# Attention and maxout on one core: first banks, weight differences and row sums put in another order

## The chip, the cores and the metric

The kernel runs on one core of one Trainium2 chip. The core has a matrix engine (TensorE, PE in the profile; its weight loads are shown apart as PEld), VectorE (DVE), ScalarE (ACT), GpSimd (POOL) and SyncE (SP). The engines run side by side, each through its own list of instructions in a fixed order, and wait for each other by semaphores. Transfers run on 16 DMA engines and are issued here by POOL and SP. TensorE writes its products to PSUM, which has eight banks of 128 partitions by 512 fp32 numbers; another engine must read a bank out before TensorE may fill it again. SBUF is the on-chip memory from which all engines read.

The metric is the device time of one execution in microseconds (us).

## The reference

The input is q, k, v of 8 batches, 8 heads, 1024 positions and 64 channels, two projections E and F of 64 x 1024, and three weights. Linformer attention is followed by a two-way maxout layer, all in fp32:

```python
k_proj = einsum('ks,bhsd->bhkd', E, k)      # 1024 positions -> 64
v_proj = einsum('ks,bhsd->bhkd', F, v)
scores = (q @ k_proj^T) / 8                 # 1024 x 64 for each head
attn   = exp(scores - max) ; attn /= sum(attn) + 1e-9
x      = (attn @ v_proj), heads side by side  # 8192 tokens x 512
out    = maximum(x @ w1, x @ w2) @ w_out      # 512 -> 1024 -> 512
```

## The kernel before, in words

The maxout is rewritten: maximum(x w1, x w2) is relu(x (w1 - w2)) + x w2. So the kernel forms `wd_sb` = w1 - w2, does an "up" product with it and a relu into `gt_sb`, and a "down" product of `gt_sb` with w_out, to which x times `m_sb` is added, where `m_sb` = w2 w_out is computed once. Most products use seven block products in place of eight (Strassen's scheme), so DVE forms sums of blocks (`sum_s`, line 655, and `sub4`, line 546) and adds of results. Batch 0's up product is done plainly, in eight blocks of 128 features (`fb`) for each of two halves j of the tokens.

The order of the work on every engine is written out by hand (`manual_schedule`). A list `slots` gives the order of the products, and `at_slot(key, step, ...)` hangs further steps behind a slot. Key ("P", n, p, i) is piece i of down product p of unit n; there are 16 units, two for each batch. What stands earlier in program order stands earlier in the list of each engine that it uses.

PSUM is shared out by name. Four single banks, `mm0` to `mm3`, are handed out by `mm_bank()` in the rotation `turn`; `mm_bank(n=...)` takes one by number and leaves the rotation alone. `att_banks()` hands out two pairs in rotation. A bank is handed out again only when the last reader of its old content is done.

The parts that the change touches:

- `up_slots` (line 473; matmuls on line 481, relu on line 490, for `fb` 3 on DVE on line 492). `u0` are the blocks of j = 0, `u1` those of j = 1. The first two blocks of each are begun with the first two of their four 128-row steps (`r1=2`), in the order u0[0], u1[0], u0[1], u1[1]; so these four open the four single banks, in that order. Later they are finished (`r0=2`) in the order u0[0], u0[1], u1[0], u1[1], and then come u0[2], u0[3], u1[2], u1[3], two double transposes of w2 (`step_w2t`), u0[4], u0[5], and so on, each taking the next bank in the rotation.
- `step_wd(f0, r0, r1, n)` (line 496, instruction on line 497): DVE's difference w1 - w2, for columns f0 to f0 + n and rows r0 to r1 of the four row groups. `wd_sb` has the columns 0 to 255 done in three calls, then columns 256, 512 and 768 on, 256 at a time and all four row groups in one instruction of 128 x 1024.
- The weights come in blocks by POOL's queue (lines 124 and 133). From column 256 on each block is split by z: with row group r = 2g + z, one transfer brings row groups 0 and 2, the next 1 and 3.
- `step_at(t, g, j, att, between)` (line 390): 16 small matmuls with the value projections (line 346) and two DVE multiplications by the inverse row sums (line 401), whose result is half of x. With `between`, that step is put between the two multiplications; batch 0's last call has `step_wd(0, 2, 4)` there.
- `step_w2t` (line 501): eight TensorE transposes (line 506) and an ACT copy (line 512).
- Batch 1's attention is spread over unit 0's down product by a table of names: `qt` is the transposing of queries, `sc` scores and their exponential (lines 334 and 374), `dn` row sums on TensorE and their logarithm on ACT (lines 346 and 382), `in` the exponential that inverts them (line 386), `at` the values. The two digits are the head group g and the half j. Unit 0's down products come in the order p1, p2, p6, p5, p7, p3, p4, in two pieces each (matmuls on line 787). Entry 12 of the table stands behind p3's second piece, entry 13 behind p4's first, entry 14 behind p4's second, whose result ACT then copies out (line 891), and entry 15 behind unit 1's first piece.
- Batch 2's queries are transposed by DMA (line 317, SP's queue). Its first scores stand in unit 1 and wait for that transfer.

Of the kernel before, what the change touches and what calls it, by code (L numbers as in the profile page):

```python
# [12 lines left out]
ALU = mybir.AluOpType  # L13
# [3 lines left out]
def kernel(  # L17
# [12 lines left out]
    nc = tc.nc  # L30
# [4 lines left out]
    DF = moe_w1.shape[1]  # L35
# [3 lines left out]
    NDC = DM // 128  # L39
# [17 lines left out]
    turn = [0, 1, 2, 3]  # L57

    def mm_bank(dtype=FP32, n=None):
        if n is None:  # L60
            n = turn.pop(0)
            turn.append(n)
        return ps.tile([128, 512 if dtype == FP32 else 1024], dtype, tag=f"mm{n}", name="mm_ps")

    def att_banks(dtype=FP32):
        return ps.tile(
            [128, 2, 512 if dtype == FP32 else 1024], dtype, tag="att", bufs=2, name="att_ps"
        )
# [4 lines left out]
    def big(n, dtype=FP16):  # L73
        return const.tile([128, 16384 // mybir.dt.size(dtype) // 2], dtype, tag=f"big{n}", name=f"big{n}")
# [44 lines left out]
    w1_sb = big(1).rearrange("p (r f) -> p r f", r=NDC)  # L119
    w2_sb = big(2).rearrange("p (r f) -> p r f", r=NDC)  # L120
    wo_sb = const.tile([128, NFB, DM], FP16, tag="wo", name="wo_sb")
    for g in range(2):
        for w_sb, w in ((w2_sb, moe_w2), (w1_sb, moe_w1)):
            nc.gpsimd.dma_start(
                out=w_sb.rearrange("p (g z) f -> p g z f", z=2)[:, g, :, 0:256],
                in_=w.rearrange("(g p z) f -> p g z f", p=128, z=2)[:, g, :, 0:256],
            )
    for w_sb, w, f0, f1 in (
# [3 lines left out]
        for z in range(2):  # L132
            nc.gpsimd.dma_start(
                out=w_sb.rearrange("p (g z) f -> p g z f", z=2)[:, :, z, f0:f1],
# [221 lines left out]
    def values_into(t, g, j, at_ps):  # L356
        for z in range(2):
            tiles_into(
                lambda o: at_ps[o][:, z * W : (z + 1) * W], t["ex", g, j],
                lambda rows, hh: vp_of(t, 4 * g + hh, rows, z),  # L360
            )

    def new_xt(t):
        t["xt"] = xpool.tile([128, NP2, 2, HALF], FP16, tag="xt", name="xt_sb")

    def x_out(t, g, j):
        return t["xt"][:, 2 * g : 2 * g + 2, :, j * W : (j + 1) * W]
# [20 lines left out]
    def step_at(t, g, j, att=False, between=None):  # L388
        if "xt" not in t:
            new_xt(t)  # L390
        ld = t.pop(("ld", g, j))
        if att:
            both = att_banks()
            at_ps = [both[:, o, :] for o in range(2)]
        else:
            at_ps = [mm_bank() for _ in range(2)]
        values_into(t, g, j, at_ps)
        for o in range(2):
            if o and between is not None:
                between()  # L400
            nc.vector.tensor_tensor(
                out=x_out(t, g, j)[:, :, o, :],
                in0=at_ps[o].rearrange("q (z n) -> q z n", z=2),
                in1=ld[:, o, None, :].broadcast_to([128, 2, W]),
                op=ALU.mult,
            )
# [61 lines left out]
    wd_sb = const.tile([128, NDC, DF], FP16)  # L468
# [4 lines left out]
    def up_slots(t, j):  # L473
        t["gt", j] = gt = gpool.tile([128, NFB, HALF], FP16, tag="gt", name="gt_sb")
        for fb in range(NFB):
            def up(fb=fb, r0=0, r1=NDC):
                if r0 == 0:
                    t["up", j, fb] = mm_bank()
                h_ps = t["up", j, fb]
                for r in range(r0, r1):  # L480
                    nc.tensor.matmul(  # L481
                        out=h_ps,
                        lhsT=wd_sb[:, r, fb * 128 : (fb + 1) * 128],
                        rhs=t["xt"][:, r, :, j * W : (j + 1) * W],
                        start=(r == 0), stop=(r == NDC - 1),
                    )
                if r1 < NDC:
                    return
                if fb != 3:
                    nc.scalar.activation(out=gt[:, fb, :], in_=h_ps, func=ACTF.Relu)  # L490
                else:
                    nc.vector.tensor_scalar_max(gt[:, fb, :], h_ps, 0.0)
            yield up


    def step_wd(f0, r0=0, r1=NDC, n=256):
        nc.vector.tensor_tensor(
            out=wd_sb[:, r0:r1, f0 : f0 + n], in0=w1_sb[:, r0:r1, f0 : f0 + n],
            in1=w2_sb[:, r0:r1, f0 : f0 + n], op=ALU.subtract,
        )  # L500

    def step_w2t(f0, att=False):
        ps_t = att_banks(FP16)[:, 0, :] if att else mm_bank(FP16)
        for f in range(2):
            for r in range(NDC):
                nc.tensor.transpose(
                    out=ps_t[:, (f * NDC + r) * 128 : (f * NDC + r + 1) * 128],
                    in_=w2_sb[:, r, f0 + f * 128 : f0 + (f + 1) * 128],
                    identity=ident16,
                )  # L510
        fb = f0 // 128
        nc.scalar.copy(  # L512
            out=w2t_sb[:, fb : fb + 2, :].rearrange("q f m -> q (f m)"), in_=ps_t
        )
# [389 lines left out]
    t = tiles[0]  # L904
# [38 lines left out]
    for f0 in (0, 128):  # L943
        step_wd(f0, 0, 2, 128)
    step_at(t, 1, 0, True)
    u0, u1 = [*up_slots(t, 0)], [*up_slots(t, 1)]
    step_at(t, 1, 1, True, between=lambda: step_wd(0, 2, 4))
    for i in range(2):
        for u in u0, u1:
            u[i](r1=2)  # L950
# [2 lines left out]

    load_all(tiles[1], 1, "k", k)
    wt = [lambda f0=f0: step_w2t(f0) for f0 in range(0, DF, 256)]
    wd = [lambda f0=f0: step_wd(f0) for f0 in range(0, DF, 256)]
    f = lambda s, *a: lambda: s(tiles[0], *a)

    def loads(b, *names):
# [54 lines left out]
    def at_slot(key, s, *a):  # L1014
        steps.setdefault(key, []).append(lambda: s(*a))
# [11 lines left out]
    t = tiles[1]  # L1027
    at_slot((0, 22), new_attn, t)
    at_slot((0, 22), lambda: turn.__setitem__(slice(None), [2, 3]))
    for n, x in enumerate((  # L1030
        "", "", "", "", "", "kv", "", "kpt", "qt00 qt10", "", "sc00 sc10", "qt01", "qt11",
        "dn00 in00 dn10", "in10", "at00 AT10 sc01",
    )):
        key = ("P", n // 15, (n - 1) // 2 % 7, (n - 1) % 2) if n else (0, 22)
        for name in x.split():
            if name[0] == "k":
                if name == "kpt":
                    at_slot(key, step_kpt_sets, t)
                else:
                    at_slot(key, step_kv_sets, t)  # L1040
                    at_slot(key, loads, 2, "v", "q")
            else:
                g, j = int(name[2]), int(name[3])
                s_ = {"qt": step_qt, "sc": step_sc,
                      "dn": step_dn, "in": step_inv, "at": step_at, "AT": step_at}[name[:2]]
                args = (4 * g, 4, 2 * j, 2 * j + 2) if name[:2] == "qt" else (g, j)
                at_slot(key, s_, t, *args, *([True] if name[:2] == "AT" else []))
        if n in (1, 5):
            at_slot(key, step_t, 1, (0, 1) if n == 1 else (2, 3))
        if n in (2, 3):  # L1050
            for i in range(2):
                at_slot(key, step_tw, 2 * (n - 2) + i)
        if 6 <= n < 10:
            at_slot(key, sums_x, U[0, 1], ((2, 0, 1, 3)[n - 6],))


    t = tiles[2]
# [8 lines left out]
    for b in range(3, B):  # L1066
        t = tiles[b]
        n = 2 * b - 3
# [13 lines left out]
    for i, (new, old) in enumerate(zip([*groups[1:], none], groups)):  # L1082
        n, h = divmod(i + 2, 2)
# [72 lines left out]
```

## Time and profile before

| what | us |
|---|---|
| time, median of 3 runs (lowest to highest) | 320.96 (320.38 to 321.17) |
| the profiled execution's own time | 320.5 |
| its span (first to last instruction) | 318.7 |
| PE busy | 312.2 (98%) |
| PEld busy | 253.5 (80%) |
| DVE busy | 239.6 (75%) |
| ACT busy | 205.8 (65%) |
| POOL busy | 40.7 (13%) |

The page gives busy times and shares of the span; the chain of waits goes back from the last instruction, at each step to what released it. A matmul's row is longer than the time that it holds the engine, since the next starts before it ends: 32 matmuls of 128x512 in a row took 6.91 us in the chain, 0.216 each, while one has a row of 0.38. Times "at" are us from the span's start. The granted TensorE clock was 1.00 in every stretch looked at.

### The profile page before, as it was taken

What the parts mean: (1) busy time and instruction counts of PE and PEld (TensorE: products, weight loads), DVE (VectorE), ACT (ScalarE), POOL (GpSimd) and SP (SyncE); (2) the same over time, 40 slices, a digit from 0 to 9 for tenths busy, and PEclk for the clock granted to TensorE, in tenths of its full rate; (3) what the DMA queues carried; (4) which work ended last, traced back from release to release, by engine and by line L of the source; (5) the groups of instructions that cost most, each with busy time, mean ns of one, the idle gap of its engine ahead of it and who ended that gap; (6) DMA issues with size and microseconds to landing.
All of it is one profiled execution on the core that took longest, in us unless ns stands there. A gap on an engine that the chain in (4) does not pass through costs nothing.

```text
span 318.7 us, 9176 instructions
## 1 busy us (share of the span) xinstructions
PE 312.2 (98%) x3920; PEld 253.5 (80%) x3920; DVE 239.6 (75%) x435; ACT 205.8 (65%) x372; POOL 40.7 (13%) x63
## 2 busy tenths in 40 slices
PE   7989999999999999999999999999999999999996
PEld 3654588788887888788887888788887888888885
DVE  2365889886969696896969696996969696969683
ACT  2476742767876777477776777477776777765541
POOL 8359002004000300030000400031000000000000
PEclk9999999999999999999999999999999999999999
DMA  7999999999979899899989899989979131303124
GB/s 189 203 199 180 203 206 202 207 161 159 207 141 178 167 210 245 209 191 170 234 191 217 163 199 245 221 154 174 231 150 214 45 102 35 101 33 102 35 99 132
DMA packets 76424, 53.41 MB, mean 168 GB/s; under 512 B 29536, under 2 KB 76000, under 8 KB 76384
## 3 DMA queue, kind: packets, MB, share of 16 engines
q0 software_dynamic: 30688, 28.05, 56.2%
q1 hardware_dynamic: 45408, 24.58, 32.1%
q8 instruction: 30, 0.49, 0.6%
q10 hardware_dynamic: 288, 0.20, 0.2%
q14 instruction: 10, 0.08, 0.1%
HBM read 57.15 MB, written 16.78 MB: 232 GB/s over the span
## 4 chain that ended last, share of the span: by engine, by line
PE 91%; DMA 4%; ACT 2%; POOL 1%; issue 0%; DVE 0%; POOLq 0%; DVEq 0%
PE mm_ps L787 47%; PE mm_ps L695 27%; DMA v_sb<-in_v_dram 4%; PE mm_ps L481 4%; PE att_ps L346 3%; PE mm_ps L189 3%; PE mm_ps L334 2%; PE mm_ps L583 2%; PE att_ps L231 1%; ACT big L512 1%; PE mm_ps L305 1%; POOL k_sb L102 0%; ACT gt_sb L490 0%; POOL q_sb L102 0%; ACT ld_sb L382 0%; PE att_ps L334 0%
## 5 line engine op out<-in xcount | busy, mean ns | idle before, releaser
L669 ACT COPY p_sb<-mm_ps 128x512 f32<-128x512 f32 x179 | 101.8, 592 | 49.5 <-PE mm_ps L695 27.7
L787 PEld LDWEIGHTS <-big 128*128 128x128 f16 x768 | 73.6, 98 | 11.8 <-issue 3.6
L787 PE MATMUL mm_ps<-T_sb,big 128*128 128x256 f16 x576 | 76.9, 273 | 0.0
L710 DVE TENSOR_TENSOR gt_sb<-mm_ps,p_sb 128x512 f16<-128x512 f32 x56 | 38.5, 688 | 44.8 <-PE mm_ps L695 44.5
L695 PE MATMUL mm_ps<-big,big 128*128 128x256 f16 x336 | 50.4, 273 | 0.0
L695 PEld LDWEIGHTS <-big 128*128 128x128 f16 x448 | 43.8, 98 | 5.1
L787 PE MATMUL mm_ps<-wo_sb,gt_sb 128*128 128x256 f16 x256 | 42.6, 273 | 0.0
L787 PEld LDWEIGHTS <-gt_sb 128*128 128x128 f16 x376 | 35.6, 98 | 6.7 <-issue 2.7
L427 ACT ACTIVATE ex_sb<-mm_ps 128x512 f16<-128x512 f32 x50 | 27.2, 597 | 17.7 <-PE mm_ps L334 12.3
L695 PEld LDWEIGHTS <-wd_sb 128*128 128x128 f16 x336 | 32.9, 98 | 3.8
L695 PE MATMUL mm_ps<-xt_sb,wd_sb 128*128 128x256 f16 x224 | 32.8, 273 | 0.0
L456 DVE TENSOR_TENSOR xt_sb<-att_ps,ld_sb 128x1024 f16<-128x1024 f32 x26 | 31.7, 1219 | 0.2
L297 POOL COPY junk<-qt_sb 1x1 f16<-1x1 f16 x6 | 2.5, 420 | 174.8 <-DMA qt_sb<-q_sb 174.8
L787 PE MATMUL mm_ps<-m_sb,xt_sb 128*128 128x256 f16 x128 | 24.5, 273 | 0.0
L817 DVE TENSOR_TENSOR o_sb<-mm_ps,p_sb 128x512 f32<-128x512 f32 x32 | 21.9, 683 | 2.8 <-ACT p_sb L846 2.0
L713 DVE TENSOR_SCALAR gt_sb<-gt_sb 128x512 f16<-128x512 f16 (+1 forms) x60 | 20.9, 348 | 2.1
L655 DVE TENSOR_TENSOR big<-gt_sb 128x1024 f16<-128x1024 f16 x32 | 21.8, 683 | 0.0
L787 PE MATMUL mm_ps<-wo_sb,big 128*128 128x256 f16 x128 | 21.5, 273 | 0.0
L756 ACT ACTIVATE gt_sb<-mm_ps 128x512 f16<-128x512 f32 x28 | 16.8, 601 | 5.7 <-PE mm_ps L695 5.7
L787 PE MATMUL mm_ps<-T_sb,gt_sb 128*128 128x256 f16 x120 | 20.3, 273 | 0.0
L787 PEld LDWEIGHTS <-xt_sb 128*128 128x128 f16 x188 | 18.3, 98 | 2.3 <-issue 0.2
L710 DVE TENSOR_TENSOR gt_sb<-p_sb 128x512 f16<-128x512 f32 x28 | 19.1, 682 | 0.6 <-ACT p_sb L669 0.6
(112 smaller groups left out, 431.8 us busy)
## 6 DMA issues: line engine op xcount, KB each, us to landing
out_dram<-o_sb SPq DMA_DIRECT2D x62, 256.0 KB, 2.8
k_sb<-in_k_dram POOLq DMA_DIRECT2D x7, 1024.0 KB, 10.0
v_sb<-in_v_dram POOLq DMA_DIRECT2D x7, 1024.0 KB, 16.2
q_sb<-in_q_dram POOLq DMA_DIRECT2D x5, 1024.0 KB, 23.4
q_sb<-in_q_dram POOLq DMA_DIRECT2D x6, 512.0 KB, 16.5
big<-in_moe_w_dram POOLq DMA_DIRECT2D x12, 128.0 KB, 6.8
v_sb<-in_v_dram POOLq DMA_DIRECT2D x4, 256.0 KB, 13.5
wo_sb<-in_moe_w_out_dram POOLq DMA_DIRECT2D x1, 1024.0 KB, 11.2
```

Source lines behind the costliest of these rows:

```text
L189: nc.tensor.matmul(out=kv_ps[r * KP : (r + 1) * KP, h * D : (h + nh) * D], lhsT=eft[i][:, c, :], rhs=t[w][:, h0 + h : h0 + h + nh, c, :], ...
L427: nc.scalar.activation(out=t["ex", g, j][:, e, :], in_=banks[e], func=ACTF.Exp, scale=scale)
L456: nc.vector.tensor_tensor(out=x_out(t, g, j).rearrange("q z o n -> q o z n"), in0=at_ps.rearrange("q o (z n) -> q o z n", z=2), in1=ld[:, ...
L481: nc.tensor.matmul(out=h_ps, lhsT=wd_sb[:, r, fb * 128 : (fb + 1) * 128], rhs=t["xt"][:, r, :, j * W : (j + 1) * W], start=(r == 0), stop= ...
L655: nc.vector.tensor_tensor(out=S(i), in0=S(0) if x is None else x, in1=y(), op=op)
L669: copy(out=x, in_=bank)
L695: nc.tensor.matmul(out=bank[:, m * W : (m + 1) * W], lhsT=w_[:, n_, (2 * d + m) * 128 : (2 * d + m + 1) * 128], rhs=a[:, n_, :], start=(n ...
L710: nc.vector.tensor_tensor(out=c_blk(j, c), in0=two(x), in1=two(y), op=ALU.add)
L713: nc.vector.tensor_scalar_max(ap, ap, 0.0)
L756: nc.scalar.activation(out=out, in_=in_, func=ACTF.Relu)
L787: nc.tensor.matmul(out=bank[i][:, 0:CH] if two_banks else bank[:, i * CH : (i + 1) * CH], lhsT=a(c)[:, i * 128 : (i + 1) * 128], rhs=w_(c) ...
L817: nc.vector.tensor_tensor(out=o_sb, in0=two(x), in1=two(y), op=ALU.add)
```

## The change

Four edits:

1. The four blocks that batch 0 begins first take their banks by number. The order in which they are begun is the same, but u0[0] and u0[1] take the first two banks of the rotation and u1[0] and u1[1] the last two. Before, u1[0] had the second and u0[1] the third.
2. `step_wd(0, 2, 4)` is placed ahead of both multiplications of batch 0's last `step_at`, not between them.
3. The weight differences of columns 512 and 768 are done in two instructions each, one for the row groups 0 and 2 and one for 1 and 3.
4. In batch 1's table, `dn00 in00 dn10` goes from entry 13 to entry 12 and `in10` from entry 14 to entry 12. TensorE has the 16 row-sum matmuls ahead of p4's first piece and not between its pieces; ACT has the inversion `in10` ahead of the copy of p4 and not behind it.

TensorE, ACT, POOL and SP keep their instructions in number and shape; DVE has two more. SP's and POOL's lists are the same.

```diff
@@ up_slots
                 if r0 == 0:
-                    t["up", j, fb] = mm_bank()
+                    t["up", j, fb] = mm_bank(n=None if r1 == NDC else first_banks[j][fb])
@@ new, behind step_wd
+    def step_wd_rows(f0):
+        for z in range(2):
+            rows = lambda w: w.rearrange("p (g z) f -> p g z f", z=2)[:, :, z, f0 : f0 + 256]
+            nc.vector.tensor_tensor(
+                out=rows(wd_sb), in0=rows(w1_sb), in1=rows(w2_sb), op=ALU.subtract
+            )
@@ batch 0
     step_at(t, 1, 0, True)
     u0, u1 = [*up_slots(t, 0)], [*up_slots(t, 1)]
-    step_at(t, 1, 1, True, between=lambda: step_wd(0, 2, 4))
+    step_wd(0, 2, 4)
+    step_at(t, 1, 1, True)
+    first_banks = turn[0:2], turn[2:4]
     for i in range(2):
         for u in u0, u1:
             u[i](r1=2)
...
-    wd = [lambda f0=f0: step_wd(f0) for f0 in range(0, DF, 256)]
+    wd = [lambda f0=f0: step_wd(f0) for f0 in range(0, 512, 256)]
+    wd += [lambda f0=f0: step_wd_rows(f0) for f0 in range(512, DF, 256)]
@@ batch 1's table
-        "", "", "", "", "", "kv", "", "kpt", "qt00 qt10", "", "sc00 sc10", "qt01", "qt11",
-        "dn00 in00 dn10", "in10", "at00 AT10 sc01",
+        "", "", "", "", "", "kv", "", "kpt", "qt00 qt10", "", "sc00 sc10", "qt01",
+        "qt11 dn00 in00 dn10 in10", "", "", "at00 AT10 sc01",
```

## The prediction, written before the changed kernel was run

> **What bounds the kernel now.** I read the shares of the page first, then the waits of TensorE, then the chain of waits and the timeline round each wait found.
>
> ```profile
> PE 312.2 (98%) x3920; PEld 253.5 (80%) x3920; DVE 239.6 (75%) x435; ACT 205.8 (65%) x372; POOL 40.7 (13%) x63
> ...
> PE 91%; DMA 4%; ACT 2%; POOL 1%; issue 0%; DVE 0%; POOLq 0%; DVEq 0%
> ```
>
> TensorE is the bound: 98% busy and 91% of the chain. The change leaves its instructions alone, so only holes between them can be won or made. The answer on the whole run's waits of TensorE has seven groups, 3.5 us together; of these the edits can reach one, and the chain shows what it hangs on:
>
> ```profile
> PE mm_ps L481 <- ACT gt_sb L490: 0.3, 1, 0.3
> ...
> 25.59 1.01 ACT big L512
> 26.60 0.99 ACT gt_sb L490 x2
> 27.59 0.91 ACT big L512
> 28.49 0.51 ACT gt_sb L490
> 29.00 0.04 issue
> 29.05 2.75 PE mm_ps L481 x12
> ```
>
> For 3.4 us the end hangs on ACT, not TensorE: a copy of w2, the relus of u0[0] and u0[1], a second copy, the relu of u1[0]. Behind that one TensorE starts u0[3] at 29.05, because u0[3] takes u1[0]'s bank. The weight differences of that stage wait for transfers:
>
> ```profile
> 25.33 0.68 DVE L401 TENSOR_TENSOR xt_sb<-att_ps,ld_sb 128x512 f16<-128x512 f32 x1
> ...
> 26.93 0.69 DVE L497 TENSOR_TENSOR wd_sb<-big,big 128x1024 f16<-128x1024 f16 x1 [0.92 <-DMA big<-in_moe_w_dram]
> 27.68 0.76 PEld L481 LDWEIGHTS <-wd_sb 128*128 128x128 f16 x5 [0.36 <-DVE wd_sb L497]
> ...
> 31.33 0.69 DVE L497 TENSOR_TENSOR wd_sb<-big,big 128x1024 f16<-128x1024 f16 x1 [0.53 <-DMA big<-in_moe_w_dram]
> 31.94 0.69 DVE L492 TENSOR_SCALAR gt_sb<-mm_ps 128x512 f16<-128x512 f32 x1
> ```
>
> In batch 1's stage, the timeline shows a second, smaller hole, and later a transfer that lands shortly before its use:
>
> ```profile
> 60.34 0.58 ACT L382 ACTIVATE ld_sb<-att_ps 128x512 f32<-128x512 f32 x1
> 60.57 0.40 PE L346 MATMUL att_ps<-ex_sb,vp_sb 64*32 64x256 f16 x16
> 60.97 0.41 PE L334 MATMUL att_ps<-qt_sb,kpt_sb 64*32 64x256 f16 x16
> ...
> 72.61 0.71 POOL L297 COPY junk<-qt_sb 1x1 f16<-1x1 f16 x1 [19.96 <-DMA qt_sb<-q_sb]
> 73.12 0.14 PEld L334 LDWEIGHTS <-kpt_sb 64*32 64x32 f16 x16 [0.21 <-issue]
> ```
>
> **1, the banks: -0.49.** The eight matmuls from 26.79 start 0.216 apart; the last of u0[2] starts at 28.34, so u0[3] could start at 28.56. It starts at 29.05: 0.49 lost (the 0.3 of the wait counts from the modelled end of the row before). In the changed kernel u0[3] takes u0[1]'s bank, whose relu ran from 26.98 to 27.58: no wait. What is late next: u1[2] now waits for u1[0]'s relu (end 28.99) and would start at 29.42; u1[3] for u1[1]'s relu (28.84 and 0.65: 29.49), wanted at 30.29; the transposes for u0[2]'s bank (ACT, 29.98), wanted at 31.15; all in time. Bounds 0 and -0.49; I take the whole.
>
> **2, the difference ahead of the multiplications: 0.** DVE would run `step_wd(0, 2, 4)` at 24.40 instead of 25.00, if its last weight block is there: issued at 15.51 with 8.5 to landing, so 24.0. u0[0]'s second half would then follow the transposes (last start 25.33, 0.056 each) at 25.39, not 25.47: -0.08. But u0[2] needs the columns from 256 on, whose block lands just before 26.93; its first weight load stays at 27.68, and the 0.08 is lost there. The multiplication now queued behind `step_wd` starts 0.33 later, but the second still ends at 26.01; the next transposes, at 26.26, wait for both: 0.25 of cover. If that is gone, because the block lands after 24.65, the loss grows with the delay until the wait at 27.68 absorbs it. Bounds -0.08 and +0.1 (26.01 and a start 0.33 later is 26.34, 0.08 past 26.26); I take 0.
>
> **3, the row halves: 0, but they keep step 1.** With 0.49 won, u0[4]'s first weight load comes at 31.98, not 32.47. The old instruction would end at 32.02; with 0.06 for the semaphore (27.62 to 27.68) that loses 0.10. The halves have the size of the 0.42 row of 128x512. The first needs the transfer before the last one (issued 23.75 with 6.8: 30.55) and ends near 31.0; the second starts at 31.33 and ends at 31.75, in time. DVE pays 2 x 0.42 - 0.69 = 0.15 each; behind it stand u1[3]'s relu, 0.2 sooner than now, and the last difference, wanted only 3.5 us later. Bounds: 0, and +0.10 if a half costs the full 0.69 of the whole.
>
> A rule to weigh against two more DVE instructions while POOL issues loads: POOL's issue at 31.73, beside the DVE row at 31.33, took 0.87, and the one at 28.66 with DVE idle 0.87. The Trainium skill (SBUF — State Buffer, section "SBUF: two separate sides") says that a DVE operation in a two-port mode keeps GpSimd from writing descriptors; its section "Who interferes with whom" exempts tensor_tensor. By the row nothing is lost; by the page's rule in its wide form batch 2's k load would be issued up to two halves, 0.84, later, and it lands at 58.5 (31.73 and 26.8) for a use at 66.1, so the sum is the same by both.
>
> **4, the row sums: -0.17.** The scores `sc01` want the bank pair of `dn10`'s logarithm, which ends at 60.92; 16 small matmuls hold TensorE 0.23 (60.34 to 60.57), so they could start at 60.80 and start at 60.97. Moved up by p4's first piece (58.05 to 58.80), `dn10`'s logarithm ends near 60.2. New waits: `dn10` now stands at about 58.2 and needs the exponential that ends at 57.82; ACT's copy of p4 has the inversion ahead of it (0.63) but starts about when it does now, 60.8, as the two logarithms came earlier; its bank is wanted after 62. DVE's multiplications at 61.01 stand behind full DVE rows from 57.88 on, so they gain nothing. Bounds 0 and -0.2.
>
> **What takes part of it back: +0.14.** Batch 2's first scores load weights at 73.12, and would at 72.46. They need the DMA transposes issued at 66.82, with 5.7 to landing: 72.52, and POOL, which waits for the same, went on at 72.61. So they start at 72.6. That landing should not move with TensorE: the DMA engines are busy in every slice from 50 to 67, and the query load before it (issued 51.15, 15.7 to landing) queues behind others. Other landings leave room: wo at 37.96 for 38.95, batch 1's v at 28.66 + 19.5 = 48.16 for 49.3, its q at 50.7 for 52.4. Bounds 0 and +0.66.
>
> After that all stages are a TensorE stream with no wait left, so what is won stays: -0.49 - 0.17 + 0.14 = -0.52. The profiled execution would go from 320.5 to 320.0; it stands 0.46 under the median of 320.96, so the forecast is 320.44, said as 320.4.
>
> **The rivals.** One measurement of this kernel can tell some 0.3% (0.96 us) from no change.
>
> *More than the holes of this trace.* The median is 0.46 slower than the execution profiled. If that 0.46 is lost in the stage from 26 to 33, by weight blocks and relus coming later, and halves and banks take it out too, the gain is 0.49 + 0.17 + 0.46 = 1.12: 319.8. For it: this stage waits for transfers at three places. Against: a difference waits for its block in both kernels.
>
> *The transfer hides it.* If the 0.46 is instead waiting for batch 2's queries, TensorE already stands there in most executions, and an earlier arrival gains nothing: 321.0. For it: 0.5 of slack behind 20 us of transfers. Against: the profiled execution shows no wait there.
>
> *Slower.* The same place decides: TensorE reaches batch 2's scores at 73.12 now, and if in the changed kernel their queries land after 74.1, it is over 0.96 later than before. Landing times of such transposes reach 6.6 (here 5.7), which gives 73.4; the query load would have to be 0.7 later as well, behind v and q loads that POOL issues 0.49 sooner into a full queue. Price: 322.3. Against: nothing in the change adds a transfer.
>
> **How the numbers follow.** Forecast 0.42; hidden by the transfer 0.18; more than the holes 0.25; slower 0.15. The first two are within 0.3% (0.60), the third faster, the fourth slower. The range, 319.5 to 321.9, leaves out the slower case (0.15) and the far end of the faster one (0.05). The forecast's own range is 320.3 (-0.66) to 320.9 (-0.1).
>
> **What would show it.** Right: no wait of L481 on L490 and u0[3] 0.216 behind u0[2]; two DVE rows of about 0.42 ending near 31.75; scores behind 16 values without a hole; batch 2's scores at about 72.6. Wrong: a weight load at u0[4] that waits for DVE; a wait of the transposes before u1[0]; a wait for queries of over 0.3.

## The result, and the profile after

The median fell from 320.79 us (22 runs, 320.38 to 321.17) to 320.11 us (22 runs, 319.73 to 322.19). The ratio is 0.9983, with a 95% interval of 0.9975 to 0.9992: 0.55 us less (0.0017 x 320.8), between 0.26 and 0.80; the two medians differ by 0.68. That is within 0.3%, and below 1 by its interval. Here and below, the few runs above 322 us of kernels without added work (the changed kernel's 322.19 is one; its other runs are 320.90 or less) have a granted clock of 0.989 to 0.995, all others with a clock on record 0.998 or more, so they tell nothing about the edits. The profiled execution took 319.73 us; before it was 320.5.

The page of the changed kernel (its span; busy time and share of each engine; the chain of waits by engine):

```profile
span 318.0 us, 9177 instructions
PE 312.1 (98%) x3920; PEld 253.5 (80%) x3920; DVE 240.4 (76%) x437; ACT 206.1 (65%) x372; POOL 40.0 (13%) x63
PE 92%; DMA 4%; POOL 1%; ACT 1%; DVE 0%; issue 0%; POOLq 0%; DVEq 0%
```

TensorE is as busy as before and the span 0.7 shorter. So holes between its instructions went. DVE is 0.8 busier; its two further instructions account for 0.3 of that at most.

The chain of waits of the changed kernel, from the first transposes of w2 (columns: start and duration in us, engine, tensor and line, number of instructions; `up_slots` is still line 481, the transposes are now line 513, the down products 794):

```profile
25.10 0.45 PE att_ps L513 x8
25.55 0.86 PE mm_ps L481 x4
26.41 0.45 PE att_ps L513 x8
26.86 4.40 PE mm_ps L481 x20
31.25 0.89 PE mm_ps L513 x16
32.15 6.91 PE mm_ps L481 x32
```

Before, this stretch of the chain went through ACT for 3.4 us. Now it is TensorE all the way, and the 20 matmuls from u1[0]'s second half to u1[3] take 4.40, where 20 x 0.216 is 4.32. The 0.08 that is left is u0[2] waiting for its weight difference, as the timeline shows on DVE and PEld (columns as in the chain; in brackets, the idle time of the engine before the row and what ended it):

```profile
26.88 0.69 DVE L497 TENSOR_TENSOR wd_sb<-big,big 128x1024 f16<-128x1024 f16 x1 [0.87 <-DMA big<-in_moe_w_dram]
27.62 3.14 PEld L481 LDWEIGHTS <-wd_sb 128*128 128x128 f16 x16 [0.40 <-DVE wd_sb L497]
...
30.17 0.42 DVE L505 TENSOR_TENSOR wd_sb<-big,big 128x512 f16<-128x512 f16 x1
30.77 0.43 DVE L505 TENSOR_TENSOR wd_sb<-big,big 128x512 f16<-128x512 f16 x1 [0.18 <-DMA big<-in_moe_w_dram]
31.29 0.69 DVE L492 TENSOR_SCALAR gt_sb<-mm_ps 128x512 f16<-128x512 f32 x1
```

The halves have the 0.42 of a 128x512 row, and the second still waits for its transfer. In batch 1's stage, the same view:

```profile
59.15 0.58 ACT L382 ACTIVATE ld_sb<-att_ps 128x512 f32<-128x512 f32 x1
...
60.03 0.40 PE L346 MATMUL att_ps<-ex_sb,vp_sb 64*32 64x256 f16 x16
60.25 0.40 PE L334 MATMUL att_ps<-qt_sb,kpt_sb 64*32 64x256 f16 x16
...
71.68 0.18 POOL L297 COPY junk<-qt_sb 1x1 f16<-1x1 f16 x1 [19.57 <-DMA qt_sb<-q_sb]
72.39 0.14 PEld L334 LDWEIGHTS <-kpt_sb 64*32 64x32 f16 x16 [0.21 <-issue]
```

The second logarithm now ends at 59.73, half a microsecond ahead of the scores, which start 0.22 behind the value products and not 0.40. Batch 2's queries had landed by 71.68, and their scores load weights at 72.39 without a wait.

Two lengths make the executions comparable, whatever their transfers did before. Length A runs from the first transposes of w2 to u0[4]'s first matmul (timeline starts), before and then after:

```profile
24.94 0.61 PE L506 MATMUL att_ps<-ident,big 128*128 128x128 f16 x8
...
32.52 1.67 PE L481 MATMUL mm_ps<-xt_sb,wd_sb 128*128 128x512 f16 x7
...
24.94 0.61 PE L513 MATMUL att_ps<-ident,big 128*128 128x128 f16 x8
...
31.98 2.32 PE L481 MATMUL mm_ps<-xt_sb,wd_sb 128*128 128x512 f16 x10
```

That is 7.58 before and 7.04 after. Pure matmul time there is 0.45 + 0.86 + 0.45 + 4.32 + 0.89 = 6.97. Length B runs from batch 1's first scores to the first scores of unit 1 (the chain's entries), before and then after:

```profile
55.35 0.56 PE att_ps L334 x32
...
63.67 0.34 PE mm_ps L334 x16
...
54.81 0.56 PE att_ps L334 x32
...
62.94 0.34 PE mm_ps L334 x16
```

That is 8.32 before and 8.13 after. Between and behind them nothing moved: from u0[4] to batch 1's first scores is 22.66 in both, from unit 1's first scores to batch 2's 9.53 and 9.52 (all by the chain's entries). The gain in the trace is 0.54 + 0.19 = 0.73.

### The profile page after: what moved, and what is told of

Same layout as the page of the kernel before. It is cut to its first block, busy times and chain, and to the rows that moved or that the text cites. A ratio compares the mean times of both kernels' runs of the same rounds, so it can differ in the third digit from the quotient of the medians.

```text
span 318.0 us, 9177 instructions
## 1 busy us (share of the span) xinstructions
PE 312.1 (98%) x3920; PEld 253.5 (80%) x3920; DVE 240.4 (76%) x437; ACT 206.1 (65%) x372; POOL 40.0 (13%) x63
## 4 chain that ended last, share of the span: by engine, by line
PE 92%; DMA 4%; POOL 1%; ACT 1%; DVE 0%; issue 0%; POOLq 0%; DVEq 0%
PE mm_ps L794 47%; PE mm_ps L702 27%; PE mm_ps L481 4%; DMA v_sb<-in_v_dram 4%; PE att_ps L346 3%; PE mm_ps L189 3%; PE mm_ps L334 2%; PE mm_ps L590 2%; PE att_ps L231 1%; PE mm_ps L305 1%; POOL k_sb L102 0%; POOL q_sb L102 0%; ACT ld_sb L382 0%; ACT ex_sb L374 0%; DVE o_sb L892 0%; PE att_ps L513 0%
## 5 line engine op out<-in xcount | busy, mean ns | idle before, releaser
L297 POOL COPY junk<-qt_sb 1x1 f16<-1x1 f16 x6 | 1.5, 246 | 175.1 <-DMA qt_sb<-q_sb 175.1
```

## The experiments

My theory was the one on record: u0[3]'s wait for a bank (0.49) and the scores' wait for a bank pair (0.17) go, a little comes back at batch 2's queries. The rivals were that the halves and the moved difference carry the gain, that the queries hide or limit it, and that the first profile had lucky transfers. Times beside a kernel are medians on the same chip as the kernel before.

### Each edit alone, and each left out

The banks alone: the kernel before with

```diff
-                    t["up", j, fb] = mm_bank()
+                    t["up", j, fb] = mm_bank(n=None if r1 == NDC else first_banks[j][fb])
...
     step_at(t, 1, 1, True, between=lambda: step_wd(0, 2, 4))
+    first_banks = turn[0:2], turn[2:4]
```

> The kernel before with the banks alone changed. My theory: u0[3] starts 0.216 us behind u0[2]'s last matmul, 0.49 sooner; u0[4]'s first weight load then waits some 0.1 for the whole weight difference that ends near 32.0; so TensorE is 0.35 to 0.45 us ahead at the end of the up blocks, and the time is 0.3 to 0.5 us less. Rival (the banks are not the cause: ACT's relus merely end at that time): u0[3] still waits, no gain. Rival (the halves and the moved difference carry the gain): under 0.15 us.

320.10 us against 320.62, ratio 0.9991 (0.9980 to 1.0002). The interval includes 1, so the times alone do not show the gain; the lengths do. Length A is 7.05: 0.53 less than before. The chain:

```profile
25.63 0.95 PE mm_ps L481 x4
27.03 4.32 PE mm_ps L481 x20
32.24 6.91 PE mm_ps L481 x32
```

The 20 matmuls have no hole at all. The wait of u0[4] for the whole difference, which I expected to take back 0.1, isn't there. Length B is 8.33, unchanged.

The banks left out: the changed kernel with `mm_bank()` as before.

> The changed kernel with the old banks, all other edits kept. My theory: u0[3] waits for u1[0]'s relu and starts near 29.05, as in the kernel before; what is left is the row sums' 0.17 us, so the time is 0.1 to 0.25 us under the kernel before. Rival (the other edits carry the gain): 0.4 us or more under it.

320.50 us against 320.62, ratio 0.9993 (0.9980 to 1.0007). Length A is 7.59, B is 8.13. One row of the timeline of TensorE says it:

```profile
29.26 2.75 PE L481 MATMUL mm_ps<-xt_sb,wd_sb 128*128 128x512 f16 x12 [0.40 <-ACT gt_sb L490]
```

The wait for ACT's relu is back, and all of length A's gain is gone, although the halves and the moved difference are in place. So the banks are its cause, and the other two edits alone are worth nothing in this stage.

The row sums alone: the kernel before with the new table, `"qt11 dn00 in00 dn10 in10", "", "", "at00 AT10 sc01"`.

> The kernel before with batch 1's row sums alone put earlier. My theory: the scores follow the value products at once, 0.17 us sooner; at batch 2's scores TensorE arrives at 72.95, after the queries' landing of 72.5, so all of it stays: 0.17 us less, 0.1 to 0.25. Rival (ACT's copy behind the inversion holds the next product): no gain, or a new wait of a matmul behind that copy.

320.52 us against 320.62, ratio 1.0001 (0.9993 to 1.0010): too small for the times. In the chain, the two entries that bound length B:

```profile
55.59 0.56 PE att_ps L334 x32
...
63.72 0.34 PE mm_ps L334 x16
```

8.13, 0.19 less than before; A is 7.58, unchanged. The row sums at their old places in the changed kernel mirror it:

> The changed kernel with batch 1's row sums at their old places. My theory: the scores wait 0.17 us for the bank pair of the second logarithm, and the time is 0.1 to 0.2 us above the changed kernel. Rival (batch 2's queries set the time at 72.5 whatever comes before): TensorE waits there in the changed kernel but not here, and the times are equal.

320.16 us, ratio 0.9974 (0.9955 to 0.9993); A 7.03, B 8.33. The times can't show 0.19 us; the lengths do, in both directions, and in all kernels below B is 8.13 or 8.14 with the new table.

The halves left out: the changed kernel with `step_wd(f0)` for all four column blocks.

> The changed kernel with the last two weight differences whole again. My theory: u0[4]'s first weight load waits for a difference that ends near 32.0 and TensorE loses 0.1 us there, 0.05 to 0.15 where the last transfer lands as it did; the time is 0.1 us above the changed kernel. Rival (the halves carry nothing, DVE is in time anyway): no wait of a weight load there. Rival (the halves cost: two DVE instructions more): the end of the up blocks is sooner than in the changed kernel.

320.03 us against 320.71, ratio 0.9981 (0.9971 to 0.9991). Length A is 7.04, as with the halves. On the timeline:

```profile
31.45 1.06 PE L513 MATMUL mm_ps<-ident,big 128*128 128x128 f16 x16
...
31.58 0.69 DVE L497 TENSOR_TENSOR wd_sb<-big,big 128x1024 f16<-128x1024 f16 x1 [0.96 <-DMA big<-in_moe_w_dram]
32.34 1.89 PE L481 MATMUL mm_ps<-xt_sb,wd_sb 128*128 128x512 f16 x8
```

The whole difference ends at 32.27, and u0[4] starts at 32.34 (its first weight load at 32.32), where the 16 transposes leave off (31.45 + 16 x 0.056). It was in time by a hair, after a block that came as late against its predecessor as in the profile before (4.35 from one wait's end to the other's; 4.40 before, 3.89 in the first profile after). The expected 0.1 was not lost.

The moved difference left out: the changed kernel with `step_wd(0, 2, 4)` between the multiplications.

> The changed kernel with the second weight difference between the two multiplications again. My theory: u0[0]'s second half starts 0.08 later (25.47, not 25.38), and the 0.08 is taken up at u0[2], which waits for its own difference until 27.6 in both; no difference in time. Rival: the 0.08 stays and the whole stage behind it is 0.08 later.

319.93 us against 320.71, ratio 0.9979 (0.9969 to 0.9990). The chain:

```profile
25.73 0.96 PE mm_ps L481 x4
27.14 4.49 PE mm_ps L481 x20
```

u0[0]'s second half starts 0.53 behind the transposes and not 0.44, as expected, and the hole at u0[2] is 0.17. From the start of the difference that u0[2] waits for to u0[4]'s entry in the chain is 27.25 to 32.52, 5.27, the same as after (26.88 to 32.15): so the moved difference is worth nothing there, and the longer A (7.23) is that block landing later.

### The changed kernel again

> The changed kernel once more, for a second profile of it. My theory (the holes behind the banks and ahead of batch 1's scores are gone, 0.49 and 0.17, and up to 0.14 comes back at batch 2's scores when its queries land at 72.5): 0.5 to 0.7 us under the kernel before, TensorE's plain up blocks without a wait from u0[2] on, and batch 2's first scores at 72.4 to 72.7. Rival (the first profile was a lucky one, its transfers all 0.3 to 0.9 us early): batch 2's scores wait visibly, 0.2 us or more, and the time is within 0.2 us of the kernel before.

320.02 us against 320.62, ratio 0.9988 (0.9979 to 0.9997). A is 6.97, with no wait of u0[2] left, B 8.14. POOL passed batch 2's queries at 71.88, TensorE loaded weights at 72.54.

> The changed kernel, to stand beside the one with three differences halved on the same chip, and for a third profile. 0.5 to 0.7 us under the kernel before by the holes; batch 2's first scores without a wait, or with up to 0.2 us where the queries land late.

320.09 us against 320.69, ratio 0.9976 (0.9959 to 0.9994). A is 7.08, B 8.14; queries by 71.99, scores at 72.54. So the first profile wasn't alone: in three of three, TensorE reached the scores 0.55 to 0.71 after the queries were there. Three profiles do not exclude a wait. With the banks alone POOL passed the queries at 72.60, and with three differences halved and the second one at its old place (below) at 72.52; queries that late would have held the changed kernel, which loads weights at 72.39 to 72.54, by up to 0.2 (an estimate from these times).

### Batch 2's queries: what sets their landing, and what it costs to be late

The kernel before, with ten matmuls of 128x512 that nobody reads put ahead of the last m product:

```diff
+    for n in range(2):
+        at_slot((0, 21), warm, 5, True)
```

> The kernel before with ten matmuls of 128x512 that nobody reads (2.16 us of TensorE) put ahead of p4 of the m product, before batch 1's projections; every step behind them is 2.16 later, the POOL issues of batch 2's v and q loads among them (52.4 and 53.3 instead of 50.3 and 51.2). My theory (batch 2's queries land when the full transfer queue lets them, not when they are issued): the transposes are still issued at 66 to 67 and TensorE reaches the scores at 75.3. Rival (the landing follows the issue): the transposes are issued near 69.0, 2.16 later. The time is 2.1 us more by both.

322.87 us (one run), 2.2 above the kernel before. On the timeline:

```profile
53.53 1.50 POOL L102 DMA_DIRECT2D q_sb<-in_q_dram  x2
67.03 6.05 SPq L317 DMA_TRANSPOSE qt_sb<-q_sb  x2
73.15 0.18 POOL L297 COPY junk<-qt_sb 1x1 f16<-1x1 f16 x1 [18.11 <-DMA qt_sb<-q_sb]
75.50 0.14 PEld L334 LDWEIGHTS <-kpt_sb 64*32 64x32 f16 x16 [0.21 <-issue]
```

The loads were issued 2.38 later than before (51.15), and the transposes, which wait for the first of these loads, only 0.21 later (66.82). The rival, 2.16 later, is out: the queue, much more than the issue, sets when that load lands. POOL passed the transposed queries at 73.15, 0.54 later than in the kernel before (72.61) and later than in any other kernel without more load; whether the late issue has a part in that, one run can't tell.

The changed kernel with 512 KB of load put ahead of those queries. It has 12 output buffers in place of 14.

```diff
+            elif (b_, n) == (2, "v"):
+                load_all(tiles[2], 2, "v", v)
+                spare = const.tile([128, H // 2, NC, D], FP16, tag="spare", name="spare_sb")
+                nc.gpsimd.dma_start(
+                    out=spare, in_=k[2, 0 : H // 2].rearrange("h (p c) d -> p h c d", c=NC)
+                )
```

> The changed kernel with a load of 512 KB that nobody reads put ahead of batch 2's queries on POOL's queue (and 12 output buffers in place of 14, to make room). My theory (the place where it could turn slower): the queries land 2.9 us later, as long as 512 KB took before, their transposes are issued near 69, TensorE waits some 2.2 us at batch 2's first scores near 72.5 and the time is 1.9 to 2.4 us above the changed kernel, 1.3 to 1.8 above the kernel before. Rival (the transposes are paced by something else, or the queue has room): the scores wait less than 0.5 us.

321.18 us (one run). The chain, from POOL's issue to the scores:

```profile
51.79 17.37 DMA q_sb<-in_q_dram
69.16 0.02 issue
69.18 4.54 DMA qt_sb<-q_sb
73.72 0.14 issue
73.85 0.41 PE mm_ps L334 x16
```

The transposes were issued 2.4 to 3.2 later than in the three profiles of the changed kernel (66.01, 66.14 and 66.75), about as expected, and now their landing, not TensorE, is on the chain. But the first transposes, which these scores need, took 4.54 to land (4.59 to POOL's passing), against 5.1 to 6.1 to POOL's passing in the other kernels, so the wait was smaller than my 2.2: from u0[4] to these scores is 32.59 to 73.85, 41.26, against 40.31 after, so 0.95. Neither the 2.2 nor the rival's under 0.5 was met. The fewer output buffers show no cost of their own: the stage of the up blocks starts 0.08 later, length A is 0.37 longer, and with the 0.95 that is 1.40, the whole difference of the two spans (319.4 and 318.0).

This execution showed a second thing, on the timeline of DVE and TensorE:

```profile
25.00 0.43 DVE L497 TENSOR_TENSOR wd_sb<-big,big 128x512 f16<-128x512 f16 x1 [0.44 <-DMA big<-in_moe_w_dram]
...
26.77 0.61 PE L513 MATMUL att_ps<-ident,big 128*128 128x128 f16 x8 [0.25 <-DVE xt_sb L401]
```

Here the last weight block of the first quarter landed at 24.9. The moved difference stood waiting for it, both multiplications stood behind the difference, and the second transposes behind the multiplications. From the next difference's start (27.07) to u0[4]'s entry (32.59) is 5.52, 0.25 more than 5.27. It was the only one of the eight profiles with the moved difference (after included) in which it waited.

### The hole that is left

The changed kernel with the difference of columns 256 to 511 in halves too:

```diff
-    wd = [lambda f0=f0: step_wd(f0) for f0 in range(0, 512, 256)]
-    wd += [lambda f0=f0: step_wd_rows(f0) for f0 in range(512, DF, 256)]
+    wd = [lambda: step_wd(0)]
+    wd += [lambda f0=f0: step_wd_rows(f0) for f0 in range(256, DF, 256)]
```

> The changed kernel with the difference of columns 256 to 511 in row halves as well. In the profiles so far u0[2] waits for that difference, and TensorE has a hole of 0 to 0.17 us there. My theory: the second half ends 0.27 sooner than the whole did (0.42 behind the last block and not 0.69) and the hole is gone; 0 to 0.15 us less than the changed kernel, its six blocks from the second transposes on then taking 4.32 us (20 x 0.216) in the chain and not 4.32 to 4.49. Rival: the first half is late too, or DVE's second instruction delays u0[3]'s relu; no change or a longer stage.

319.94 us against 320.69, ratio 0.9976 (0.9955 to 0.9997); the changed kernel in the same comparison had 320.09 and the same ratio. The chain:

```profile
26.56 0.45 PE att_ps L513 x8
27.01 4.32 PE mm_ps L481 x20
31.33 0.89 PE mm_ps L513 x16
```

A is 6.97, all matmul. The hole is gone, and the times can't tell the two kernels apart.

This execution also shows what the halves of columns 512 are for (DVE, then TensorE):

```profile
30.91 0.43 DVE L505 TENSOR_TENSOR wd_sb<-big,big 128x512 f16<-128x512 f16 x1 [0.58 <-DMA big<-in_moe_w_dram]
31.59 0.43 DVE L505 TENSOR_TENSOR wd_sb<-big,big 128x512 f16<-128x512 f16 x1 [0.26 <-DMA big<-in_moe_w_dram]
...
32.06 1.24 PE L481 MATMUL mm_ps<-xt_sb,wd_sb 128*128 128x512 f16 x5
```

Here the last block of columns 512 held DVE until 31.59. The second half ended at 32.02, and u0[4], whose first matmul needs the first half alone, started at 32.06. A whole difference could not have started before 31.59; with its 0.69 it would have ended at 32.28, 0.22 past u0[4]'s start (an estimate from these rows).

The same with the second difference between the multiplications again:

> The changed kernel with three differences halved, and the second difference between the two multiplications again. In the kernel with three halved no wait is left between the first transposes of w2 and u0[4]: 6.97 us, all of it matmuls. My theory (the 0.08 us that the earlier difference wins is lost only because u0[2] waits anyway): with that wait gone, the old place costs its 0.05 to 0.08 us, 7.02 to 7.05, and no more than that in time. Rival (it is worth nothing in any case): 6.97.

320.00 us against 320.75, ratio 0.9978 (0.9969 to 0.9987). The chain:

```profile
25.79 0.96 PE mm_ps L481 x4
27.19 4.32 PE mm_ps L481 x20
```

A is 7.05. With u0[2]'s wait gone, the 0.08 of the moved difference reaches the end of the stage, as expected. In the kernel as changed it is lost at u0[2] in the first and third profiles, which have a hole there (0.08 and 0.11), and kept in the second, which has none (A is 6.97).

All runs together (A and B in us, from the profile of each; the ratio is to the kernel before):

| kernel | time | ratio, 95% | A | B |
|---|---|---|---|---|
| before | 320.79 | | 7.58 | 8.32 |
| after | 320.11 | 0.9983 (0.9975 to 0.9992) | 7.04 | 8.13 |
| after, second profile | 320.02 | 0.9988 (0.9979 to 0.9997) | 6.97 | 8.14 |
| after, third profile | 320.09 | 0.9976 (0.9959 to 0.9994) | 7.08 | 8.14 |
| banks alone | 320.10 | 0.9991 (0.9980 to 1.0002) | 7.05 | 8.33 |
| row sums alone | 320.52 | 1.0001 (0.9993 to 1.0010) | 7.58 | 8.13 |
| without the banks | 320.50 | 0.9993 (0.9980 to 1.0007) | 7.59 | 8.13 |
| without the row sums | 320.16 | 0.9974 (0.9955 to 0.9993) | 7.03 | 8.33 |
| without the halves | 320.03 | 0.9981 (0.9971 to 0.9991) | 7.04 | 8.14 |
| without the moved difference | 319.93 | 0.9979 (0.9969 to 0.9990) | 7.23 | 8.13 |
| three halved | 319.94 | 0.9976 (0.9955 to 0.9997) | 6.97 | 8.13 |
| three halved, difference between | 320.00 | 0.9978 (0.9969 to 0.9987) | 7.05 | 8.13 |
| before, ten matmuls more (one run) | 322.87 | | 7.58 | 8.32 |
| after, 512 KB more (one run; B by timeline starts) | 321.18 | | 7.41 | 8.13 |

## Why the prediction was right, point by point

**The total.** I forecast 0.52 less and no measurable difference by 0.3%. The ratio gives 0.55 less, with 0.26 to 0.80 round it, the medians 0.68 and the traces 0.73. That 0.55 lies so near 0.52 is partly luck: the interval holds 0.73 as well, and of the forecast's terms the take-back did not come. In absolute terms the forecast was 320.44 and the median is 320.11; 0.17 of that gap is the kernel before, whose median was 320.96 over three runs and 320.79 over 22.

**Step 1, the banks, -0.49: right.** From the start of u0[2]'s difference to u0[4]'s entry in the chain is 5.76 before and 5.27 after, just 0.49. Over all runs it is 5.76 to 5.86 in the four profiles with the old banks and 5.27 to 5.30 in the seven with the new ones that keep that difference whole, the one whose first block came late left out; with the old banks the end hangs on ACT and not on that difference, so there it moves with the block. The waits that I named as next in line did not show.

**Step 2, the moved difference, 0: right in two of three profiles; one of its bounds was reached and the other passed.** The 0.08 was there and was lost at u0[2], as the kernel with three halved shows by removing that loss; in the second profile of the changed kernel u0[2] had no hole and the 0.08 was kept, which is the lower bound. On the other side, the cover of 0.25 ran out in one execution, when the block landed at 24.9, past the 24.65 that I gave; I bounded the loss at 0.1 and it was 0.25. The bound was too narrow: I let the block be late by one place in DVE's order, not by the whole of its delay.

**Step 3, the halves: 0 in the sum, right; "they keep step 1" holds in one run, but the 0.10 was not lost where I put it.** Two inputs of that 0.10 failed. The step took u0[4]'s weight load (31.98) as the time by which the difference must be there; without the halves the difference ended 0.07 before u0[4]'s first matmul and 0.05 before its load (32.32), and nothing was lost. And it took one execution's start of that difference (31.33, when its last block was there) as the time. In the three profiles of the changed kernel DVE took that block up at 30.77, 30.89 and 30.92; a whole difference would have ended by 31.61, in time, and the second half ended at 31.20 to 31.35 and not near 31.75. In the kernel with three halved the block came at 31.59, and there the halves kept some 0.2. In the other eight profiles with the halves a whole difference, begun when the last block was there, would have been in time too. So they are a cover against a late block. The delay of POOL's issues that I weighed did not come: beside the halves two issues took 1.75 and the next 0.90, and batch 2's k load was issued at 31.58, against 31.73 before.

**Step 4, the row sums, -0.17: right in mechanism, a little small.** It is 0.19 or 0.20 (8.32 or 8.33 against 8.13 or 8.14) in every pair of kernels that differs in it.

**The take-back, +0.14: wrong in size; it is 0 in all three profiles of the changed kernel.** What failed is that I took one execution's landing (72.52 to 72.61) as the landing. POOL passed it at 71.68, 71.88 and 71.99 in those three, and between 71.93 and 73.15 in the other kernels without the extra load. The margin of the changed kernel is 0.55 to 0.71 in these three; with the banks alone it was down to 0.07 (72.60 against 72.67). That the landing does not follow TensorE is right as far as the transposes' issue goes: with the loads issued 2.38 later it moved by 0.21. But POOL passed at 72.39 to 72.80 in the three profiles with the old banks and no added matmuls, and at 71.68 to 72.60 in the nine with the new ones and no added load, where the same loads are issued some 0.5 sooner. The two ranges overlap, so whether part of the earlier landing belongs to the change or all of it to chance stays open.

**The rivals.** "More than the holes" fell: its 1.12 lies outside the interval (0.26 to 0.80). Length A was 7.58 or 7.59 in all four profiles with the old banks, but three of those executions took 320.49 to 320.53 and the fourth had matmuls added, so what a slower one loses, and where, is not shown. Part of the difference between executions lies ahead of that stage: the first transposes of w2 started between 24.94 and 25.30 in these profiles. Where exactly is open. "The transfer hides it" fell too: no kernel without the extra load waited at batch 2's scores. The slower case did not come, but its place is real: queries whose transposes were issued about 3 us late cost 0.95 there.

What stays open is how often the late first-quarter block and late queries strike: the block was late in one of eight profiles with the moved difference. What the kernel before lost in its runs of 321.0 to 321.5 is not known either: no profile was taken of one.

## What to carry to other kernels

When buffers are handed out by rotation, look at who held the next buffer last and when that reader is done: two blocks that were begun in one order and finished in another cost half a microsecond here, by names alone. Work out a gain at the place where it arises, and then walk it down the bound engine to the next wait for a transfer, since there it can be lost (0.08 at u0[2]) or kept. And take the margin to a transfer from several executions; one trace gives one draw of its landing.

## What the runs showed of the hardware

- The landing of batch 2's first query load, behind other loads in POOL's queue, hardly depended on its issue: issued 2.38 later, the transposes that wait for it were issued 0.21 later. 512 KB put ahead of it moved them by 2.4 to 3.2.
- The same transfers land differently from run to run by as much as the edits are worth. The block that u0[2]'s difference waits for let DVE start between 26.88 and 27.25 in the profiles that keep that difference whole; counted from the first transposes of w2 that is 1.84 to 2.13.
- The first of batch 2's two DMA transposes was passed by POOL 5.1 to 6.1 after its issue in the other kernels and 4.6 (69.18 to 73.77) in the one with the extra load. No run tells why.
- A matmul started on time 0.07 after its weights' producer had ended (32.27 and 32.34), with its weight load at 32.32. The loads of u0[4] that start 0.05 ahead of their matmul (31.93 and 31.98 in the changed kernel) were earlier than that run needed.
